# Attention decode, layer 2: scores of eight kept heads laid out as 256 keys on 128 partitions instead of 512 keys on 64

## The chip, the cores and the metric

The kernel runs on one core of one Trainium2 chip. The metric is device time of one execution in microseconds (us). The span in the profile goes from the first to the last instruction of one profiled execution; the execution's time has a little more around it.

## The reference

Two layers, each an attention block (A) and an MLP mixer (B), for a single token `x` of 640 values. Both layers use the same weights and the same cache.

```python
def _A_ref(x, k_cache, v_cache, wq, wo):          # 32 heads of 192, cache 32768 long
    W = min(4096, max(256, Sk // 4))               # 4096: the last 4096 keys
    q = (x @ wq) per head
    k, v = k_cache[:, :, Sk - W:, :], v_cache[:, :, Sk - W:, :]
    p = softmax(einsum("bhqd,bhkd->bhqk", q, k) * Dh ** -0.5)
    return einsum("bhqk,bhkd->bhqd", p, v) per token @ wo

x = x + _A_ref(layernorm(x), ...)                  # layer 1 (layer == 0 in the code)
x = x + _B_ref(layernorm(x), ...)
x = x + _A_ref(layernorm(x), ...)                  # layer 2 (layer == 1 in the code)
x = x + _B_ref(layernorm(x), ...)
```

Each head of K or V in the window is 4096 x 192 bf16, 1.5 MB. One query reads all of them once per layer, so the work is mostly the reading of the cache from HBM.

## The kernel before

**Loads.** Everything big is loaded by DMAs that SP issues in one fixed order (`stream`, `layer_stream`), mostly 1.5 MB each (`load_wide`, L55). They land in twelve cells of SBUF. `take` hands out the cell that has been free longest, `give` returns one; a load into a cell waits on SP's queue until the last reader of the cell has finished, and everything behind it in that queue waits too. The loads of a layer follow the work: K of the next group of four heads between the V of the current one, then a block of `wo`.

**Kept data.** The K of heads 0 to 7, already turned, stays in eight cells from layer 1 to layer 2 (`kept`, `NKEEP = 8`), with one V (head 2), one V in PSUM and in other spare places (head 3), most of the V of head 4 in `kl` and `kx`, and one block of `wo`. Layer 2 therefore begins with V of heads 0 and 1 as its only new loads: the K of head 8 goes into the cell of the first kept head to be scored, the part of V of head 4 that was not kept into the second, K of head 9 into the third, and so on. Layer 1 runs its groups of four heads from the last to the first, layer 2 from the first to the last.

**Scores.** K comes in with 128 partitions of 32 keys each. VectorE turns it in place in 32x32 blocks (`transpose_half`, L441, two halves per head). `scores` then does, per head, `NCOL` = 6 blocks of the head's values times `NT` = 2 strips of matmuls (L526): each reads a block of 16 columns of `Qblk` as weights and streams 512 columns of K, taking every second element, and writes 16 of the 32 PSUM partitions of its strip. The four heads of a group add up into the same place, each with its own rows. So the scores of a group are 64 partitions x 512. `ST_both` is one PSUM bank of 128 x 512; `next_scores` gives its lower and its upper 64 partitions in turn, so that the next group can be scored while the current one is in softmax.

**Softmax of a group** (`softmax_steps`): `part_max` (L552, VectorE) per partition; `turn_max` (L557, TensorE) into one row; `full_max` (L562, L565); `spread_max` (L573 TensorE, L576 and the exp L579 on ScalarE, into bf16 in `o_sb`); `turn_p` (L585, VectorE turns P in blocks, onto the other 64 partitions; L587); `swap` (L599, eight matmuls that bring P into the layout for P times V, L602 copy, L607 sum); `recip` (L614, L616).

**P times V** (`pv`, L649) per head: 16 matmuls of 384 columns, on four strips of 32 PSUM partitions in turn; then a turn (L656) and `o_fold` (L663, L664). `out_proj` (L677) or `out_row` (L695) is the product with `wo`.

**Order.** The order on TensorE, VectorE, ScalarE and SP is the order of the program (`manual_schedule`). In layer 2 the query of heads 0 to 3 is projected in two halves (`qa`, `qb`, L472 to L510), head 0 is scored, the second half is finished, heads 1 to 3 are scored with the softmax scale (L410, `softmax_scale`) behind head 1 and the next query's projection behind head 2. Then, for `gi == 0`, heads 4 to 7 are scored between the softmax steps of heads 0 to 3. For `gi == 1`, the softmax of heads 4 to 7 runs, and the scores of head 8, the first head whose K was loaded in this layer, stand between `spread_max` and the projection of the following query:

```python
                    turn_max()
                    full_max()
                    spread_max()
                    S(h0, 1, ST_n, 0)
                    h1 = nxt[1][1]
                    q = None
                    if gi + 2 < len(groups):
                        q = qproj_steps(...)
                    if q:
                        q[0]()
```

Of the kernel before, what the change touches and what calls it, by code (L numbers as in the profile page):

```python
# [10 lines left out]
F32 = mybir.dt.float32  # L11
# [7 lines left out]
P = 128  # L19
# [13 lines left out]
NJ4, NGK, NM = 4, 8, 4  # L33
# [26 lines left out]
def kernel(  # L60
# [14 lines left out]
    nc = tc.nc  # L75
# [12 lines left out]
    QH = 4  # L88
# [3 lines left out]
    NT = 2  # L92
    HP = P // 2
# [35 lines left out]
    psm = ctx.enter_context(tc.tile_pool(name="psm", bufs=2, space=PSUM))  # L129
# [219 lines left out]
    Eq = Ei.rearrange("p (j b) -> p j b", j=4)  # L349
# [165 lines left out]

    def scores(h, K, ST, hq):

        ng = NGK // NT
        Q = [Qblk[:, h // QH % 2, QAT[hq] + n * QSTEP:][:, 0:QW] for n in range(NCOL)]
        T = K.rearrange("p (j g f i t) -> p g j f i t", j=NJ4, g=NGK, f=NFB, t=2)  # L520
        for f in range(NFB):
            for t in range(2):
                n = 2 * f + t
                for i in range(NT):
                    r = ST[0] + 32 * i
                    nc.tensor.matmul(  # L526
                        ST_both[r:r + QW, :].rearrange("p (g j i) -> p g j i", g=ng, j=NJ4), lhsT=Q[n],
                        rhs=T[:, ng * i:ng * (i + 1), :, f, :, t],
                        start=(hq == 0 and n == 0), stop=(hq == QH - 1 and n == NCOL - 1))

# [2 lines left out]
    nc.vector.memset(ST_both[:], 0.0)  # L533
    turn = [0]

    def next_scores():
        turn[0] += 1
        i = turn[0] % 2 * HP
        return i, ST_both[i:i + HP, :]

    def softmax_steps(n, ST, sc, space, bank=None):

        held = {}
        halves = space.bitcast(BF16)
        at, ST_ps = ST
        S, T = slice(at, at + HP), slice(HP - at, P - at)

        def part_max():  # L550
            pm = short("pm")
            nc.vector.tensor_reduce(out=pm[S, :], in_=ST_ps, op=ALU.max, axis=AX.X)  # L552
            held["pm"] = pm

        def turn_max():
            pmT_ps = psm.tile([1, HP], F32, tag="psm")
            nc.tensor.transpose(pmT_ps[0:1, :], held["pm"][S, 0:1], ident[S, S])  # L557
            held["pmT"] = pmT_ps

        def full_max():  # L560
            ngm = space[0:1, 256:256 + 2 * QH]
            nc.vector.tensor_reduce(out=ngm[:], in_=held["pmT"][0:1, :].rearrange("o (q x m) -> o x q m", q=NT, m=NM),  # L562
                                    op=ALU.max, axis=AX.XY, negate=True)
            wide = space[0:1, 306:306 + HP]
            nc.vector.tensor_scalar(  # L565
                out=wide.rearrange("o (q x m) -> o q x m", q=NT, m=NM),
                in0=ngm[:].unsqueeze(1).unsqueeze(3).broadcast_to([1, NT, 2 * QH, NM]),
                scalar1=sc[0:1, 0:1], scalar2=None, op0=ALU.mult)
            held["w"] = wide

        def spread_max():
            nb_ps = psm.tile([P, 1], F32, tag="psm")
            nc.tensor.matmul(nb_ps[S, :], lhsT=held["w"],  # L573
                             rhs=one[0:1, :], start=True, stop=True)
            nb_sb = space[S, 289:290]
            nc.scalar.copy(nb_sb[:], nb_ps[S, :])  # L576
            Pr = halves[S, 0:SW]
            lpart = space[S, 288:289]
            nc.scalar.activation(out=Pr, in_=ST_ps, func=ACTF.Exp,  # L579
                                 bias=nb_sb[:, 0:1], scale=sc[S, 0:1], accum_out=lpart[:, 0:1])  # L580
            held["Pr"], held["l"] = Pr, lpart

        def turn_p():
            held["PrT"] = halves[T, 0:SW]
            nc.vector.transpose(held["PrT"], held["Pr"])  # L585
            lh = space[S, 280:284]
            nc.vector.tensor_scalar(out=lh[:], in0=hm[S, :], scalar1=held["l"][:, 0:1], scalar2=None, op0=ALU.mult)  # L587
            held["lh"] = lh

        def swap():  # L590
            ng = NGK // NT
            if bank is None:
                PT_ps = psm.tile([P, n, NJ4, NGK], F32, tag="psm")
            else:
                PT_ps = bank[:, 0:n * NJ4 * NGK].rearrange("p (h j g) -> p h j g", j=NJ4, g=NGK)
            src = held["PrT"].rearrange("p (g j i) -> p i j g", g=ng, j=NJ4)
            for m in range(NM):
                for q in range(NT):
                    nc.tensor.matmul(PT_ps[32 * m:32 * (m + 1), :, :, ng * q:ng * (q + 1)], lhsT=Eq[T, (HP - at) // 32 + q, :],  # L599
                                     rhs=src[:, m:QW:NM], start=True, stop=True)  # L600
            PT = big.tile([P, n, NJ4 * NGK], BF16, name="PT")
            nc.scalar.copy(PT[:].rearrange("p h c -> p (h c)"), PT_ps[:].rearrange("p h j g -> p (h j g)"))  # L602
            if bank is None:
                l_ps = psm.tile([P, QH], F32, tag="psm")
            else:
                l_ps = bank[:, 512:512 + QH]
            nc.tensor.matmul(l_ps[:], lhsT=ones[S, :], rhs=held["lh"][:], start=True, stop=True)  # L607
            held["lps"] = l_ps
            return PT

        def recip():
            lq = space[:, 284:288]
# [108 lines left out]
    def attention(layer, x_cur, rs_cur, x_new, z_new, rs_new, ss_new):  # L721
# [56 lines left out]
        for step in qa[1:]:  # L778
            step()
        qb[1]()  # L780
        ST = next_scores()
        q1 = qproj_steps(groups[1][0] // QH, xc)
        for hq, h in enumerate(groups[0]):
            for half in range(2):
# [30 lines left out]
        for gi, cur in enumerate(groups):  # L815
# [6 lines left out]
            if nxt:  # L822
                part_max, turn_max, full_max, spread_max, turn_p, swap, recip = softmax_steps(
                    len(cur), ST, sc, o_words, V_bank if layer == 1 and gi > 0 else None)
                ST_n = next_scores()
                if layer == 1 and gi == 0:

                    keep = [hh for hh in nxt if hh[1] < NKEEP]
# [23 lines left out]
                else:  # L852
# [7 lines left out]
                    turn_max()  # L860
                    full_max()
                    spread_max()
                    S(h0, 1, ST_n, 0)
                    h1 = nxt[1][1]
                    q = None
                    if gi + 2 < len(groups):
# [4 lines left out]
                    if layer == 1:  # L871
                        turn_p()
                        PT = swap()
                    if pending is not None:
                        y_ps = out_row(layer, *pending, acc, gi - 1 == rows[0]) if in_row else out_proj(layer, pending)
                    if layer == 0:
# [249 lines left out]
```

## Time and profile before

| | |
|---|---|
| median of 3 runs | 513.82 us (513.09 to 517.1) |
| the profiled execution | 513.58 us, its span 511.7 us |
| mean granted TensorE clock | 0.722 |
| DMA queue q1, share of 16 engines | 98.2%, 214.02 MB |
| busy: TensorE / VectorE / ScalarE | 293.1 (57%) / 297.4 (58%) / 52.1 us (10%) |
| scores, L526 | 768 matmuls of 512 columns, 151.1 us busy |
| turning K, L441 | 112 of 1759 ns, 194.6 us busy |
| P times V, L649 | 968 records, 90.3 us busy |
| exp, L579 / maximum, L552 / turn of P, L585 | 773 / 674 / 706 ns each |

In a row of a group or of the timeline, the line number, the engine, the operation and the tiles (`out<-in`) are given; "x12" is how many instructions the row holds. In a row of a stretch of time, the columns are the stretch, its length, and for TensorE's matmuls, its weight loads, VectorE, ScalarE and GpSimd the busy us with the number of instructions; then the granted clock as a share of full speed, the busy share of the 16 DMA engines (it can pass 1 in a short stretch, since packets are counted whole) and the GB/s that ended in it. The layer boundary is near 286 us of the span: the last product of the first mixer (L1070) ends at 286.4, and the first scores of layer 2 begin at 288.75.

### The profile page before, as it was taken

What the parts mean: (1) busy time and instruction counts of PE and PEld (TensorE: products, weight loads), DVE (VectorE), ACT (ScalarE), POOL (GpSimd) and SP (SyncE); (2) the same over time, 40 slices, a digit from 0 to 9 for tenths busy, and PEclk for the clock granted to TensorE, in tenths of its full rate; (3) what the DMA queues carried; (4) which work ended last, traced back from release to release, by engine and by line L of the source; (5) the groups of instructions that cost most, each with busy time, mean ns of one, the idle gap of its engine ahead of it and who ended that gap; (6) DMA issues with size and microseconds to landing.
All of it is one profiled execution on the core that took longest, in us unless ns stands there. A gap on an engine that the chain in (4) does not pass through costs nothing. (4 is left out here: it accounts for less than half of the span.)

```text
span 511.7 us, 7558 instructions
## 1 busy us (share of the span) xinstructions
PE 293.1 (57%) x3188; PEld 141.8 (28%) x3188; DVE 297.4 (58%) x492; ACT 52.1 (10%) x173; POOL 3.7 (1%) x16
## 2 busy tenths in 40 slices
PE   1145747546275463855665885848474762726585
PEld 0011313213132231422232432414231331312254
DVE  2086686557574584567633236776777475656622
ACT  1000101010010101001010111011110101001101
POOL 2000000000000000000000000000000000000000
PEclk9995685858767686585665597775869596787855
DMA  8999999999999999999999999999999999999995
GB/s 369 430 430 428 430 444 430 439 430 412 454 432 409 438 420 424 432 417 453 428 376 413 369 422 428 437 430 439 427 416 439 438 425 430 417 433 432 423 409 215
DMA packets 12005, 214.50 MB, mean 419 GB/s; under 512 B 2564, under 2 KB 3076, under 8 KB 7428
## 3 DMA queue, kind: packets, MB, share of 16 engines
q1 hardware_dynamic: 11972, 214.02, 98.2%
q8 instruction: 25, 0.41, 0.3%
q14 instruction: 8, 0.07, 0.0%
HBM read 214.01 MB, written 0.00 MB: 418 GB/s over the span
## 5 line engine op out<-in xcount | busy, mean ns | idle before, releaser
L441 DVE STREAM_TRANSPOSE cell<-cell 128x1536 uint32<-128x1536 uint32 x112 | 194.6, 1759 | 35.5 <-DMA cell<-in_A_k_cache_dram 34.9
L526 PE MATMUL ST_ps<-cell,Qblk 128*16 128x512 bf16 x768 | 151.1, 507 | 71.4 <-DVE cell L441 53.8
L649 PE MATMUL O_ps<-cell,PT 128*2 128x384 bf16 x968 | 90.3, 405 | 8.3 <-DMA cell<-in_A_v_cache_dram 7.6
L526 PEld LDWEIGHTS <-Qblk 128*16 128x16 bf16 x768 | 45.3, 105 | 145.0 <-issue 123.4
L656 DVE STREAM_TRANSPOSE o_sb<-O_ps 128x384 f32<-128x384 f32 x62 | 35.0, 565 | 45.3 <-PE O_ps L649 45.3
L649 PEld LDWEIGHTS <-PT 128*2 128x2 bf16 x1024 | 36.7, 90 | 29.4 <-issue 21.5
L486 DVE TENSOR_TENSOR o_sb<-qT_ps,words 128x24 bf16<-128x24 f32 (+1 forms) x18 | 3.2, 179 | 51.1 <-PE qT_ps L482 28.9
L557 PE MATMUL pmT_ps<-ident,words 64*1 64x64 f32 x16 | 4.0, 252 | 48.7 <-DVE words L552 48.7
L585 DVE STREAM_TRANSPOSE o_sb<-o_sb 64x512 bf16<-64x512 bf16 x15 | 10.6, 706 | 24.6 <-ACT o_sb L579 24.6
L664 ACT ACTIVATE words<-oT_ps,words 32x6 bf16<-32x6 f32 x40 | 10.3, 257 | 143.0 <-PE oT_ps L663 83.1
L663 PE MATMUL oT_ps<-o_sb,Lq 128*32 128x6 f32 x160 | 12.5, 186 | 11.8 <-DVE o_sb L656 11.3
L573 PE MATMUL nb_ps<-words,o_sb 1*64 1x1 f32 x30 | 4.9, 230 | 24.8 <-DVE o_sb L565 24.8
L663 PEld LDWEIGHTS oT_ps<-o_sb,Lq 128*32 128x32 f32 x160 | 10.9, 128 | 22.4 <-issue 15.6
L461 PE MATMUL qr_ps<-wq_sb,words 128*1 128x384 bf16 x90 | 15.8, 514 | 0.0
L557 PEld LDWEIGHTS pmT_ps<-ident,words 64*1 64x1 f32 x16 | 1.2, 76 | 51.7 <-issue 51.7
L669 ACT ACTIVATE words<-oT_ps,words 32x6 bf16<-32x6 f32 x24 | 6.2, 257 | 92.1 <-PE ST_ps L526 64.3
L472 PE MATMUL qT_ps<-words,wq_sb 128*128 128x1 bf16 x210 | 7.2, 165 | 13.0 <-DMA wq_sb<-in_A_wq_dram 12.2
L552 DVE TENSOR_REDUCE words<-ST_ps 64x1 f32<-64x512 f32 x16 | 10.8, 674 | 5.0 <-PE ST_ps L526 4.9
L695 PE MATMUL yr_ps<-cell,words 128*1 128x320 bf16 x108 | 13.4, 406 | 0.0
L576 ACT COPY o_sb<-nb_ps 64x1 f32<-64x1 f32 x15 | 2.3, 153 | 95.3 <-PE nb_ps L573 95.3
L573 PEld LDWEIGHTS nb_ps<-words,o_sb 1*64 1x64 f32 x30 | 4.0, 189 | 27.8 <-issue 26.2
L579 ACT ACTIVATE o_sb<-ST_ps,o_sb,words 64x512 bf16<-64x512 f32 x15 | 11.6, 773 | 0.5
(161 smaller groups left out, 202.7 us busy)
## 6 DMA issues: line engine op xcount, KB each, us to landing
cell<-in_A_k_cache_dram SPq DMA_DIRECT2D x56, 1536.0 KB, 27.7
cell<-in_A_v_cache_dram SPq DMA_DIRECT2D x56, 1536.0 KB, 27.7
cell<-in_A_wo_dram SPq DMA_DIRECT2D x13, 960.0 KB, 27.7
wq_sb<-in_A_wq_dram SPq DMA_DIRECT2D x5, 1536.0 KB, 13.5
cell<-in_A_v_cache_dram SPq DMA_DIRECT2D x6, 768.0 KB, 23.7
cell<-in_B_w_dram SPq DMA_DIRECT2D x1, 1536.0 KB, 12.6
cell<-in_B_w_dram SPq DMA_DIRECT2D x2, 768.0 KB, 10.3
cell<-in_A_wo_dram SPq DMA_DIRECT2D x3, 480.0 KB, 17.0
```

Source lines behind the costliest of these rows:

```text
L441: nc.vector.transpose(Ku, Ku)
L461: nc.tensor.matmul(qr_ps[32 * i:32 * i + 1, :], lhsT=xc[:, kc:kc + 1], rhs=wq_sb[:, kc, t0 * P + i * N:t0 * P + (i + 1) * N], start=(kc == ...
L526: nc.tensor.matmul(ST_both[r:r + QW, :].rearrange("p (g j i) -> p g j i", g=ng, j=NJ4), lhsT=Q[n], rhs=T[:, ng * i:ng * (i + 1), :, f, :, ...
L552: nc.vector.tensor_reduce(out=pm[S, :], in_=ST_ps, op=ALU.max, axis=AX.X)
L573: nc.tensor.matmul(nb_ps[S, :], lhsT=held["w"], rhs=one[0:1, :], start=True, stop=True)
L579: nc.scalar.activation(out=Pr, in_=ST_ps, func=ACTF.Exp, bias=nb_sb[:, 0:1], scale=sc[S, 0:1], accum_out=lpart[:, 0:1])
L585: nc.vector.transpose(held["PrT"], held["Pr"])
L649: nc.tensor.matmul(O_ps[r:r + 2, :], lhsT=PT[:, hq, 2 * i:2 * i + 2], rhs=v_pair(V, h, 2 * i * Dh, 2 * Dh), start=(i < 4), stop=(i >= NB - 4))
L656: nc.vector.transpose(o_sb[:], O_ps.rearrange("p (e a c) -> p e c a", e=2, c=NA))
L663: nc.tensor.matmul(oT_ps[r, :], lhsT=Lq[:], rhs=o_sb[:, e, :, e], start=(e == 0), stop=(e == 1))
L664: nc.scalar.activation(oT[r, :], oT_ps[r, :], ACTF.Copy, scale=rl[r, 0:1])
L695: nc.tensor.matmul(yr_ps[32 * i:32 * i + 1, :], lhsT=oT[:, k:k + 1], rhs=wo_t[:, k * D + i * N:k * D + (i + 1) * N], start=(k == 0), stop= ...
```

## The change

For the scores of heads 0 to 3 and of heads 4 to 7 in layer 2, `next_scores` is called with 4 strips instead of 2. A strip then holds 256 keys' columns, the scores of a group are 128 partitions x 256, and the two groups have the left and the right 256 columns of the bank. Per head there are 24 matmuls of 256 columns instead of 12 of 512. The softmax steps work on 128 partitions with half the columns; P is turned in place (onto the same partitions, next to itself); `swap` has 16 matmuls instead of 8, each of half the columns. All other groups keep 64 partitions x 512. Since the scores of heads 8 to 11 (64 partitions x 512) overlap those of heads 4 to 7 (128 x 256) in the bank, the scores of head 8 move from behind `spread_max` to behind `turn_p` and `swap` (`late`).

```diff
     def scores(h, K, ST, hq):
-        ng = NGK // NT
+        at, ST_ps, nt = ST
+        ng = NGK // nt
...
-                for i in range(NT):
-                    r = ST[0] + 32 * i
+                for i in range(nt):
+                    r = 32 * i
                     nc.tensor.matmul(
-                        ST_both[r:r + QW, :].rearrange("p (g j i) -> p g j i", g=ng, j=NJ4), lhsT=Q[n],
+                        ST_ps[r:r + QW, :].rearrange("p (g j i) -> p g j i", g=ng, j=NJ4), lhsT=Q[n],
                         rhs=T[:, ng * i:ng * (i + 1), :, f, :, t],
...
-    def next_scores():
+    def next_scores(nt=NT):
         turn[0] += 1
-        i = turn[0] % 2 * HP
-        return i, ST_both[i:i + HP, :]
+        if nt == NT:
+            i = turn[0] % 2 * HP
+            return i, ST_both[i:i + HP, :], nt
+        i = turn[0] % 2 * SW // 2
+        return 0, ST_both[:, i:i + SW // 2], nt
...
-        at, ST_ps = ST
-        S, T = slice(at, at + HP), slice(HP - at, P - at)
+        at, ST_ps, nt = ST
+        np_, w = 32 * nt, 2 * SW // nt
+        S = slice(at, at + np_)
+        T, t_at = (slice(HP - at, P - at), (HP - at) // 32) if nt == NT else (S, 0)
...
-            pmT_ps = psm.tile([1, HP], F32, tag="psm")
+            pmT_ps = psm.tile([1, np_], F32, tag="psm")
...
-            wide = space[0:1, 306:306 + HP]
+            wide = space[0:1, 306:306 + HP] if nt == NT else space[0:1, w // 2:w // 2 + np_]
...
-            Pr = halves[S, 0:SW]
+            Pr = halves[S, 0:w]
...
-            held["PrT"] = halves[T, 0:SW]
+            held["PrT"] = halves[T, 0:w] if nt == NT else halves[T, w:2 * w]
...
-            ng = NGK // NT
+            ng = NGK // nt
...
-                for q in range(NT):
-                    nc.tensor.matmul(PT_ps[...], lhsT=Eq[T, (HP - at) // 32 + q, :],
+                for q in range(nt):
+                    nc.tensor.matmul(PT_ps[...], lhsT=Eq[T, t_at + q, :],
...
-        ST = next_scores()
+        ST = next_scores(4 if layer == 1 else NT)
...
-                ST_n = next_scores()
+                ST_n = next_scores(4 if layer == 1 and gi == 0 else NT)
...
                     spread_max()
-                    S(h0, 1, ST_n, 0)
+                    late = layer == 1 and gi == 1
+                    if not late:
+                        S(h0, 1, ST_n, 0)
...
                     if layer == 1:
                         turn_p()
                         PT = swap()
+                    if late:
+                        S(h0, 1, ST_n, 0)
```

More of the change, by code (lines that the diff above doesn't have):

```diff
@@ L561, in full_max @@
             ngm = space[0:1, 256:256 + 2 * QH]
-            nc.vector.tensor_reduce(out=ngm[:], in_=held["pmT"][0:1, :].rearrange("o (q x m) -> o x q m", q=NT, m=NM),
+            nc.vector.tensor_reduce(out=ngm[:], in_=held["pmT"][0:1, :].rearrange("o (q x m) -> o x q m", q=nt, m=NM),
                                     op=ALU.max, axis=AX.XY, negate=True)
-            wide = space[0:1, 306:306 + HP]
+            wide = space[0:1, 306:306 + HP] if nt == NT else space[0:1, w // 2:w // 2 + np_]
             nc.vector.tensor_scalar(
-                out=wide.rearrange("o (q x m) -> o q x m", q=NT, m=NM),
-                in0=ngm[:].unsqueeze(1).unsqueeze(3).broadcast_to([1, NT, 2 * QH, NM]),
+                out=wide.rearrange("o (q x m) -> o q x m", q=nt, m=NM),
+                in0=ngm[:].unsqueeze(1).unsqueeze(3).broadcast_to([1, nt, 2 * QH, NM]),
                 scalar1=sc[0:1, 0:1], scalar2=None, op0=ALU.mult)
@@ L597, in swap @@
             for m in range(NM):
-                for q in range(NT):
-                    nc.tensor.matmul(PT_ps[32 * m:32 * (m + 1), :, :, ng * q:ng * (q + 1)], lhsT=Eq[T, (HP - at) // 32 + q, :],
+                for q in range(nt):
+                    nc.tensor.matmul(PT_ps[32 * m:32 * (m + 1), :, :, ng * q:ng * (q + 1)], lhsT=Eq[T, t_at + q, :],
                                      rhs=src[:, m:QW:NM], start=True, stop=True)
```

## The prediction

> **What bounds the kernel now.** I read first the page, for what is busy; then stretches of time with their DMA rate, for where loads were missed; last the timeline and SP's own waits at the one place that the change can reach.
>
> The span is 511.7 us, and the transfers fill nearly all of it:
>
> ```profile
> DMA  8999999999999999999999999999999999999995
> GB/s 369 430 430 428 430 444 430 439 430 412 454 432 409 438 420 424 432 417 453 428 376 413 369 422 428 437 430 439 427 416 439 438 425 430 417 433 432 423 409 215
> ...
> q1 hardware_dynamic: 11972, 214.02, 98.2%
> ```
>
> At the 430 GB/s of most slices, 214.02 MB take 497.7 us. The other 14 us of the span are the start, the end (the last row of the second layer's mixer lands near 504.9, and 6.8 us of work follow) and the slices that are short. So an edit is worth what it changes in the stream of loads: time in which no load was in the queue, or the end behind the last one. Two slices in the middle, 376 and 369, are short. Finer stretches show where:
>
> ```profile
> 265.00:270.00 5.00, 3.52 (x60) 2.31 (x57) 1.41 (x5) 0.52 (x2) 0.00 (x0) 0.50 0.86 313
> ...
> 290.00:295.00 5.00, 5.00 (x39) 1.73 (x36) 0.43 (x3) 0.47 (x2) 0.00 (x0) 0.82 0.80 310
> 295.00:320.00 25.00, 16.84 (x223) 7.92 (x223) 12.96 (x29) 3.33 (x11) 0.00 (x0) 0.85 1.02 425
> 320.00:345.00 25.00, 15.47 (x206) 7.96 (x204) 18.58 (x26) 2.31 (x8) 0.71 (x2) 0.77 1.02 440
> 345.00:450.00 105.00, 63.67 (x640) 28.97 (x637) 70.49 (x98) 11.45 (x35) 0.00 (x0) 0.72 1.00 430
> ```
>
> (The last three columns are the granted clock, the DMA share and GB/s.) The dip at 265 lies in the first layer's last group, which the change leaves alone. The dip at 290 is the start of the second layer. Behind 295 the rate is whole again to the end phase: there the queue always holds a load, and a cell that comes free sooner buys nothing. By single microseconds the dip is this:
>
> ```profile
> 289.00:290.00 1.00, 1.00 (x8) 0.28 (x6) 0.00 (x0) 0.00 (x0) 0.00 (x0) 0.50 1.03 430
> 290.00:291.00 1.00, 1.00 (x8) 0.27 (x4) 0.00 (x0) 0.00 (x0) 0.00 (x0) 0.50 1.00 418
> 291.00:292.00 1.00, 1.00 (x9) 0.30 (x7) 0.27 (x2) 0.00 (x0) 0.00 (x0) 0.58 0.67 283
> 292.00:293.00 1.00, 1.00 (x12) 0.28 (x6) 0.00 (x0) 0.00 (x0) 0.00 (x0) 1.00 0.58 188
> 293.00:294.00 1.00, 1.00 (x10) 0.58 (x10) 0.00 (x0) 0.44 (x2) 0.00 (x0) 1.00 0.94 307
> 294.00:295.00 1.00, 1.00 (x14) 0.30 (x9) 0.15 (x1) 0.03 (x1) 0.00 (x0) 1.00 0.84 356
> 295.00:296.00 1.00, 1.00 (x34) 0.84 (x34) 0.17 (x1) 0.00 (x0) 0.00 (x0) 1.00 0.97 381
> ```
>
> 288 to 291 ran at 414 GB/s on average. From 291 to 296 the five rows move 1515 KB where 5 x 414 = 2070 would have fitted: 555 / 414 = **1.3 us lost**. The cause is a load that came late:
>
> ```profile
> 288.75 2.73 PE L526 MATMUL ST_ps<-cell,Qblk 128*16 128x512 bf16 x12 [0.27 <-DVE Qblk L510]
> ...
> 291.51 0.33 SPq L157 DMA_DIRECT2D cell<-in_A_k_cache_dram  x1
> ...
> 291.53 1.65 PE L526 MATMUL ST_ps<-cell,Qblk 128*16 128x512 bf16 x12
> ...
> 293.22 0.33 SPq L182 DMA_DIRECT2D cell<-in_A_v_cache_dram  x1
> ```
>
> and among the SP queue's waits from 286 to 307 (us in total, times, longest):
>
> ```profile
> SPq L157 <- PE Qrep_ps L493: 5.4, 1, 5.4
> ```
>
> The first load of K for head 8 needs a cell. Ten of the twelve hold kept data when layer 2 begins (eight turned K, one V, one block of wo) and two take the V of heads 0 and 1. The next cell comes free when kept head 0 has been scored, at 291.48; SP had waited 5.4 us for PE, and issues at 291.51, when the load before has almost drained. The wait is named after Qrep_ps, the PE instruction behind the scores.
>
> **The change, part by part.** *Scores of the eight kept heads (L526).* Per head 12 matmuls of 512 columns become 24 of 256; the columns streamed are the same 6144, but on four strips of 32 PSUM partitions instead of two. How wide do strips run side by side? In the first head the weight loads of a pair start 0.427 us apart (289.14, 289.56, 289.99): six pairs make 2.56, and with 0.17 for the end the 2.73 of the row. So two strips of 512 columns share 0.427 us at clock 0.50. The nearest row with four strips is L649: sixteen matmuls of 384 columns take 1.45 us at the same clock, their weight loads in fours 0.32 us apart (263.98, 264.30). Per column and strip 0.427/512 and 0.32/384 are the same 0.83 ns: four run as freely as two there. So six fours of 256 columns take 6 x 0.213 = 1.28, plus 0.17: **1.45 us instead of 2.73**, 1.28 saved at half clock. At full clock a head takes 1.46 us from its first matmul to the next user of PE (295.72 to 297.19); halved in the same way that is about 0.82, or by an issue bound from L677 (30 weight load and matmul pairs of one column in 0.90, 30 ns a pair, so 24 x 0.030 = 0.72, plus 0.17) 0.89. What the rows don't show is four strips with 16 weight columns and every second element read, as K is. Bounds: 1.45 us if they run as L649's do; 2.73 if only two run at once (12 pairs of 0.213, plus 0.17), no gain; 4.4 if each pair's weight loads stand ahead of it uncovered (0.14 us for two in the first head: 12 x 0.354, plus 0.17), a loss of 1.7. I take 1.45: in both shapes the weight loads lie inside the stream already.
>
> The Trainium skill, in "TensorE: Matmul & The Clock Gate", section "Measured speedup vs the span model", gives 3.07 times for four packed row tiles and 2.38 for three column tiles, less than the count. By 3.07 of 4 the first head would take about 1.8 us and the load would gain 0.9 rather than 1.28, so 512.7 by my sum. L649's 0.32 us per four shows the whole factor here, with column strips back to back; I go by the row.
>
> *The late load.* Its issue moves from 291.51 to 290.23. In the trace the rate falls about half a microsecond behind the issue and is recovered two later, so a load issued at 290.23 is moving before the one ahead drains. What is won is not above the 1.3 lost and not above the 1.28 of the earlier issue: I take **1.2**, since some of the loss is the slow first packets of each load.
>
> *The next loads.* Heads 1 to 7 end earlier by a sum that grows: 1.28 + 0.2 for the second head (half its columns at half clock) and 0.6 for each of six, near 5 us by the eighth. The load behind head 1 moves from 293.22 to about 291.7. All wait behind the first in a queue that runs at 425 GB/s from 295 on, so nothing is counted; without that cover the gain could grow by 25 x (1 - 425/430) = 0.3 us.
>
> *Softmax of the two groups on 128 x 256.* The maximum (L552, 674 ns for 64x512), exp (L579, 773) and the turn of P (L585, 706) read half the columns. Bounds for each: half and the whole; near 0.4, 0.5 and 0.4. The one-row steps double (L562 0.21, L565 0.24 for 64 values, so up to 0.9 together instead of 0.45), `swap` issues 16 matmuls instead of 8 (0.44 us, at most 0.88) with half the columns. Net between a gain of 1.0 and a loss of 0.9 per group, all of it on DVE, ACT and PE behind 295, where the stream covers it. No DMA is added.
>
> *The moved scores of head 8 (`late`).* With group 1 on all 128 partitions, the next scores write over columns that exp reads, so `S(h0, 1, ST_n, 0)` goes behind `turn_p` and `swap`. Before, it ran from 319.18 to 321.91, and the SP issue at 321.95 followed. Now PE does the projection first (0.95), waits for the turn of P, and does `swap` (up to 0.88) and the sum behind the cast (0.65): the scores end some 1.7 us later against the rest of the group, and behind them stand out_proj and PV, which keep their order and lose nothing in sum. SP's queue is held 1.7 us longer for that cell, but the group starts up to 5 us earlier. Nothing is late next while the loads queued there last: 6.8 us separate the issues at 315.13 and 321.95, and 320 to 345 still runs at 440 GB/s. Were that cover gone, it would cost its 1.7: 514.1.
>
> *The end.* From the last landing near 504.9 to 511.7 no instruction changes.
>
> **Sum.** The profiled execution took 513.58 us (span 511.7, 1.9 around it). 513.58 - 1.2 = 512.4. Its own time is 0.24 below the median of the three runs, 513.82, which run from 513.09 to 517.1; so a median of new runs may stand at 512.6 as well.
>
> **The rivals.** *A. The gap stays.* Four strips that read every second element of K are throttled to two, or the first load's lateness was its own start and not the cell. For it: no row shows this shape. Against it: SP's 5.4 us wait on PE. Time: 513.6, with the softmax's small change hidden.
>
> *B. The clock was not at half.* The granted clock turns to 1.00 inside 291 to 292. In executions where it turns 3 us earlier, head 0 needs 1.46 before and 0.85 after; the load comes 0.6 earlier into a gap of that size or less: 513.1. For it: the clock in the page's PEclk line changes between slices at no fixed place. Against it: PE is busy 0.73 to 0.74 of 286 to 289, and the clock is still 0.50.
>
> *C. Slower: weight loads uncovered.* 24 instead of 12, each for all 128 rows, each ahead of only 0.213 us of streaming. From the bound above head 0 ends 1.7 us later, at 293.15; the dip grows by 1.7. At full clock a head then takes 12 x (0.107 + 0.14) + 0.17 = 3.1: head 1 ends near 296.3, head 2 near 299.6, but its load is needed at 298.7 (3.7 for the first and 0.9 for the short second, from 294.1) and moves a microsecond after its issue: 1.9 more. 513.6 + 3.6 = 517.2. It decides once a four takes over 0.427 us. Against it: 0.427 and 0.32 us are the bare streams in both shapes, so the loads hide there. The same page of the Trainium skill ("Packing small matmuls", "The mechanism") says that a weight load overlaps running matmuls only where its row group differs; here all use all rows, and by that rule C holds. L526 and L649 also use all rows, and their weight loads lie inside the streams; the trace does not agree with it for column strips.
>
> *D. More than the dip.* A gain above 1.6 us needs a stretch behind 295 in which loads are missed. The rows leave 0.3. About 511.5, from that and the scatter of runs.
>
> **How the numbers follow.** Forecast 0.70, A 0.14, B 0.08, C 0.05, D 0.03. The predicted time is the forecast's 512.4, own range 511.8 to 513.0. The range takes in A and B and the half microsecond by which undisturbed runs differ from the profiled one: 511.2 to 514.6; C and part of D lie outside. About 1% (5 us) is what a measurement of this kernel can tell from no change. Faster by that would need 508.4, when bytes, start and end alone make 498 + 2 + 7 = 507: 0.01. Slower by that would need 518.7, beyond C, so only something I have not seen: 0.03. Within: 0.96.
>
> **What would show it.** Right: in the changed profile the first twelve matmuls of L526 in layer 2 are twenty-four in about 1.45 us at half clock; the L157 load of K issues 1.3 us sooner against the first scores; the DMA rate stays near 410 across the place of the dip; eight heads end about 5 us sooner while the last landing moves by 1.2 only. Wrong: a first head over 2 us, a dip of the old depth, a new dip where head 8 is scored late, or a stretch behind the dip that runs above 430.

## The result, and the profile after

The changed kernel takes 512.63 us in the median of ten executions (511.19 to 513.72), the kernel before 514.16 beside it (512.78 to 517.1). The ratio is 0.9962 [0.9944, 0.9981]: 2.0 us less, somewhere between 1.0 and 2.9 (the two medians are 1.5 apart). Run again beside 35 executions of the kernel before (median 513.54), the change gave 512.12 and 0.9977 [0.9959, 0.9995], that is 1.2 us less. Both intervals hold the predicted gain of 1.2 us. The profiled execution took 512.68 us with a span of 510.9, where 512.4 had been predicted.

Line numbers behind L526 shift: the scores are L527 now, the maximum L559, exp L586, the turn of P L592, `swap` L606. First the page of the changed kernel, the slices of the DMA and its queue:

```profile
DMA  9999999999999999999989999999999999999995
GB/s 370 431 431 428 431 441 435 436 435 413 439 433 409 435 426 439 428 408 463 428 358 413 387 451 425 424 431 428 436 427 434 432 432 431 417 443 428 417 406 217
...
q1 hardware_dynamic: 11972, 214.02, 98.4%
```

The bytes are the same. (A rate in these views counts a packet whole in the stretch in which it starts, not where it ends, as was said further up; the packets of the wide loads hold 48 KB and take 1.82 us, so a row of one microsecond is rough.) The slice with the start of layer 2 reads 387 where it read 369, and the one behind it 451 instead of 422; the slice with the first layer's dip is a little worse (358 for 376). Then stretches of the changed kernel, with the columns as before (the last three are the granted clock, the DMA share and GB/s):

```profile
290.00:295.00 5.00, 4.89 (x118) 3.05 (x106) 0.68 (x5) 0.47 (x2) 0.00 (x0) 0.80 0.98 350
295.00:320.00 25.00, 17.34 (x341) 10.23 (x343) 15.28 (x34) 3.19 (x12) 0.71 (x2) 0.85 1.02 431
320.00:345.00 25.00, 15.52 (x187) 7.89 (x188) 17.69 (x23) 3.25 (x10) 0.00 (x0) 0.77 1.01 436
```

290 to 295 moved at 310 GB/s and moves at 350 now; the engines' share there went from 0.80 to 0.98. The long rows behind 295 are alike: 431 and 436, where 425 and 440 stood. Shorter ones are not. The kernel before has a second dip just behind 295, which its row from 295 to 320 hides (the second hole that the experiments speak of is another one, behind 300). First its rows, then those of the change:

```profile
295.00:300.00 5.00, 3.88 (x56) 1.87 (x54) 1.20 (x4) 0.00 (x0) 0.00 (x0) 1.00 1.05 386
300.00:305.00 5.00, 3.86 (x39) 1.58 (x37) 2.45 (x6) 1.10 (x4) 0.00 (x0) 1.00 1.11 476
```

```profile
295.00:300.00 5.00, 3.43 (x92) 2.58 (x93) 2.38 (x9) 0.81 (x3) 0.00 (x0) 1.00 1.14 468
300.00:305.00 5.00, 3.24 (x86) 2.09 (x90) 4.61 (x12) 0.27 (x1) 0.00 (x0) 1.00 1.02 437
```

In these ten microseconds the kernel before moves 4310 KB and the change 4525, half a microsecond's worth more. The first dip by single microseconds, in the change:

```profile
291.00:292.00 1.00, 1.00 (x21) 0.43 (x13) 0.00 (x0) 0.00 (x0) 0.00 (x0) 0.51 1.30 418
292.00:293.00 1.00, 1.00 (x26) 0.75 (x26) 0.11 (x1) 0.47 (x2) 0.00 (x0) 1.00 0.96 238
293.00:294.00 1.00, 1.00 (x40) 0.93 (x38) 0.04 (x1) 0.00 (x0) 0.00 (x0) 1.00 0.80 320
294.00:295.00 1.00, 0.90 (x25) 0.50 (x17) 0.25 (x2) 0.00 (x0) 0.00 (x0) 1.00 0.88 369
295.00:296.00 1.00, 0.36 (x16) 0.40 (x19) 0.59 (x3) 0.00 (x0) 0.00 (x0) 1.00 0.99 393
```

This dip is shallower, not gone. 291 to 296 move 1738 KB, where the prediction's measure is 5 x 414 = 2070: 332 / 414 = 0.8 us are still lost, where 1.3 were. In the timeline of the changed kernel stand the new scores and the load that the first of them release:

```profile
289.01 1.46 PE L527 MATMUL ST_ps<-cell,Qblk 128*16 128x256 bf16 x24 [0.27 <-DVE Qblk L510]
...
290.52 0.33 SPq L157 DMA_DIRECT2D cell<-in_A_k_cache_dram  x1
...
293.89 0.88 PE L527 MATMUL ST_ps<-cell,Qblk 128*16 128x256 bf16 x24
...
300.19 0.89 PE L527 MATMUL ST_ps<-cell,Qblk 128*16 128x256 bf16 x24
```

Kept head 0 takes 1.46 us for 24 matmuls at clock 0.50, a head at full clock 0.88 (where the row said 1.53 before). The K of head 8 is issued 1.51 us behind the first scores instead of 2.76. The last row is head 7: it ends at 301.1, 12.1 us behind the first scores, where it ended 17.9 behind them before (near 5 us sooner had been worked out; it is 5.8). Among SP's waits of the changed kernel (us in total, times, longest), from 250 to 345, the one for this load is:

```profile
SPq L157 <- PE Qrep_ps L493: 4.1, 1, 4.1
```

It was 5.4. The softmax of the two groups has these rows among the groups of 286 to 330 (busy us, mean ns of one):

```profile
L586 ACT ACTIVATE o_sb<-ST_ps,o_sb,words 128x256 bf16<-128x256 f32 x2 | 1.1, 564 | 0.1
...
L592 DVE STREAM_TRANSPOSE o_sb<-o_sb 128x256 bf16<-128x256 bf16 x2 | 0.9, 446 | 2.8 <-ACT o_sb L586 2.8
...
L559 DVE TENSOR_REDUCE words<-ST_ps 128x1 f32<-128x256 f32 x2 | 0.8, 399 | 0.0
```

From the start of the first scores of layer 2 to the end of the span, the measure that leaves out how the first layer went, the profiles have 222.95 us before and 221.89 after.

### The profile page after: what moved, and what is told of

Its sections match the earlier page's. It is cut to its first block, busy times and chain, and to the rows that moved or that the text cites. A ratio compares the mean times of both kernels' runs of the same rounds, so it can differ in the third digit from the quotient of the medians.

```text
span 510.9 us, 7784 instructions
## 1 busy us (share of the span) xinstructions
PE 282.8 (55%) x3300; PEld 141.3 (28%) x3300; DVE 296.1 (58%) x492; ACT 51.8 (10%) x173; POOL 3.7 (1%) x16
## 4 chain that ended last, share of the span: by engine, by line
DMA 73%; PE 11%; DVE 11%; issue 2%; ACT 2%; SPq 1%; ACTq 0%
DMA cell<-in_A_v_cache_dram 38%; DMA cell<-in_A_k_cache_dram 31%; DVE cell L441 7%; PE ST_ps L527 5%; DMA cell<-in_B_w_dram 4%; PE O_ps L656 1%; DVE o_sb L663 1%; ACT o_sb L586 1%; PE y_ps L1081 1%; PE qT_ps L472 1%; DVE words L559 1%; DVE V_ps L645 1%; PE qr_ps L461 1%; SPq L55 0%; DVE Qblk L510 0%
## 5 line engine op out<-in xcount | busy, mean ns | idle before, releaser
L527 PE MATMUL ST_ps<-cell,Qblk 128*16 128x512 bf16 (+1 forms) x864 | 143.9, 468 | 76.4 <-DVE cell L441 60.4
L656 PE MATMUL O_ps<-cell,PT 128*2 128x384 bf16 x968 | 88.4, 398 | 7.9 <-DMA cell<-in_A_v_cache_dram 6.0
L527 PEld LDWEIGHTS <-Qblk 128*16 128x16 bf16 x864 | 45.1, 103 | 146.5 <-issue 124.3
L564 PE MATMUL pmT_ps<-ident,words 64*1 64x64 f32 (+1 forms) x16 | 4.0, 253 | 51.3 <-DVE words L559 51.2
L592 DVE STREAM_TRANSPOSE o_sb<-o_sb 64x512 bf16<-64x512 bf16 (+1 forms) x15 | 10.1, 671 | 23.6 <-ACT o_sb L586 23.6
L580 PE MATMUL nb_ps<-words,o_sb 1*64 1x1 f32 (+1 forms) x30 | 5.0, 234 | 25.0 <-DVE o_sb L572 25.0
L461 PE MATMUL qr_ps<-wq_sb,words 128*1 128x384 bf16 x90 | 13.9, 463 | 0.0
L559 DVE TENSOR_REDUCE words<-ST_ps 64x1 f32<-64x512 f32 (+1 forms) x16 | 10.2, 640 | 3.8 <-PE ST_ps L527 3.7
L583 ACT COPY o_sb<-nb_ps 64x1 f32<-64x1 f32 (+1 forms) x15 | 2.3, 154 | 94.0 <-PE nb_ps L580 94.0
L580 PEld LDWEIGHTS nb_ps<-words,o_sb 1*64 1x64 f32 (+1 forms) x30 | 4.2, 193 | 27.6 <-issue 26.0
L586 ACT ACTIVATE o_sb<-ST_ps,o_sb,words 64x512 bf16<-64x512 f32 (+1 forms) x15 | 11.2, 746 | 0.5
```

What stands on the lines that cost most here:

```text
L461: nc.tensor.matmul(qr_ps[32 * i:32 * i + 1, :], lhsT=xc[:, kc:kc + 1], rhs=wq_sb[:, kc, t0 * P + i * N:t0 * P + (i + 1) * N], start=(kc == ...
L527: nc.tensor.matmul(ST_ps[r:r + QW, :].rearrange("p (g j i) -> p g j i", g=ng, j=NJ4), lhsT=Q[n], rhs=T[:, ng * i:ng * (i + 1), :, f, :, t] ...
L586: nc.scalar.activation(out=Pr, in_=ST_ps, func=ACTF.Exp, bias=nb_sb[:, 0:1], scale=sc[S, 0:1], accum_out=lpart[:, 0:1])
L656: nc.tensor.matmul(O_ps[r:r + 2, :], lhsT=PT[:, hq, 2 * i:2 * i + 2], rhs=v_pair(V, h, 2 * i * Dh, 2 * Dh), start=(i < 4), stop=(i >= NB - 4))
```

## The experiments

**Theory:** the time is set by the stream of loads. The only thing that the change moves in it is the issue of the K of head 8, through the scores of kept head 0; the rest of the change is hidden. **Rivals:** the gain comes from the other shortened heads or the cheaper softmax and not from this load; or the hole in the stream is no loss at all, since the stream makes it good. Below, "K issue" is how long behind the first scores of layer 2 the K of head 8 is issued, and "to the end" goes from those first scores to the end of the span.

### The change again, and the load made late on purpose

The change unaltered:

> The changed kernel as it is, run beside the next three so that they can be set against it. Theory (the whole gain is the load of K of head 8, issued sooner, in a hole of the load stream): ratio to before 0.996 to 0.999, and from the first scores of layer 2 to the end of the span 1.0 to 1.3 us less than before's 222.95. Rival (the gain grows with the five microseconds by which the later heads end sooner, or is spread over the stages behind): more than 1.6 us less, or stretches behind 300 us with a rate above 431 GB/s.

Measured: 0.9977 [0.9959, 0.9995], K issue 1.50 us, 221.29 to the end. That is 1.7 us less than 222.95, above the 1.0 to 1.3 expected and just over the 1.6 named as the rival's sign; 300 to 305 ran at 434 GB/s, over the rival's 431 as well. Against the second profile of the kernel before (222.53, told of below) it is 1.2. So this run does not set the theory apart from the rival that the gain is spread over the heads behind. In this execution the granted clock stayed at 0.50 from 290 to 315, so all eight heads took 1.46 us each, and the time is no worse for it: what the heads save at full clock was not needed for the gain here.

Ten matmuls whose result nothing reads, ahead of the first scores:

```diff
+        if layer == 1:
+            pad_ps = psm.tile([P, 512], F32, tag="psm")
+            for i in range(10):
+                nc.tensor.matmul(pad_ps[0:32, :], lhsT=Eq[:, 0, :], rhs=wq_sb[:, 0, 0:512], ...)
         ST = next_scores(4 if layer == 1 else NT)
```

> Ten matmuls of 512 columns that nobody reads stand on TensorE ahead of the first scores of layer 2: at half clock up to 4.3 us, of which some 0.3 is hidden and some runs at full clock; all heads of the two groups still end sooner against each other than before's. Theory: the load of head 8's K is issued 3 to 4 us later than in the changed kernel, at about 294, the stream runs dry from about 292 to 295, and the time rises by nearly the same, 2.5 to 3.7 us over the changed kernel: the load has no slack. Rival (the gain lies in the later heads, and the first load only fills up what the stream could make good later): less than 1 us over the changed kernel.

Measured: 514.18 us, 1.0023 [1.0006, 1.004]; 2.1 us above the change in the medians, 2.3 in the spans. That is less than the 2.5 to 3.7 expected, and well over the rival's 1. The K of head 8 is issued at 293.32. The same single microseconds of this kernel:

```profile
291.00:292.00 1.00, 1.00 (x13) 0.38 (x12) 0.00 (x0) 0.00 (x0) 0.00 (x0) 0.50 0.44 176
292.00:293.00 1.00, 1.00 (x20) 0.54 (x18) 0.00 (x0) 0.00 (x0) 0.00 (x0) 0.73 0.09 37
293.00:294.00 1.00, 1.00 (x28) 0.62 (x25) 0.27 (x2) 0.00 (x0) 0.00 (x0) 1.00 0.00 0
294.00:295.00 1.00, 1.00 (x30) 0.81 (x26) 0.00 (x0) 0.43 (x2) 0.00 (x0) 1.00 0.93 160
295.00:296.00 1.00, 1.00 (x42) 0.76 (x30) 0.15 (x1) 0.03 (x1) 0.00 (x0) 1.00 0.80 319
```

The stream runs dry, and most of what it loses there reaches the end (1378 KB too little against 2070, 3.3 us, where the second profile of the change lost 0.3); the rival that the stream makes it good falls. The ten matmuls hold up every head and load behind them too, but counted packet by packet the loss lies in the first 8 us behind the first scores (3.5 of 3.6 us), before the next loads are due. The rows also show what a load needs when nothing is ahead of it: issued at 293.32, its first packet starts at 294.28, 160 GB/s in the microsecond from 294, 319 in the next, 406 from 296 on. Its first thirteen packets take 1.0 to 1.3 us each, later ones of the same 12 KB 0.46. The full rate comes some 2.7 us behind the issue. That would explain the dip that is left after the change: the load is issued at 290.52, the ones ahead end near 292, and the rate is low until the new one is up.

### An extra load into the hole

480 KB that nobody needs, loaded between the V of head 1 and the K of head 8, in the kernel before and in the changed one. By itself it takes 480 / 430 = 1.1 us of the stream:

```diff
+        if (layer, h) == (1, NKEEP):
+            src = A_v_cache[0, VX, s0:Sk, :].rearrange("(p j) d -> p (j d)", p=P)
+            nc.sync.dma_start(kl[:], src[:, FREE - VN:FREE - NKX * Dh])
         t = take(("k", layer, h))
```

> The kernel before with one more load: 480 KB of V of head 4 are loaded again into the place where they already lie (kl), issued by SP just ahead of the load of head 8's K, where it waits for nothing. It is 0.23% more bytes, 1.14 us of stream at 430 GB/s. Theory: the stream has a hole of 1.3 us at that place, so the load runs in the hole and costs 0 to 0.3 us. Rival (no real hole: the low rate comes from the form of the loads around it): it costs its full 1.1 us.

> The same extra load of 480 KB in the changed kernel, in which the load of head 8's K comes before the stream is dry. Theory: the hole is closed, so it costs 0.7 to 1.1 us from the first scores of layer 2 to the end (the lower value if the slow first packets of K of head 8 leave part of the hole). Rival: as in the kernel before, 0 to 0.3.

Measured: in the kernel before 513.21 us, 0.9998 [0.9979, 1.0016], and 222.69 to the end, where the two profiles of that kernel (the second is told of below) have 222.95 and 222.53. The extra load costs nothing that can be seen, and by the interval less than its full 1.1 us. Its profile shows that it fills the hole: counted packet by packet, the twelve microseconds from the first scores on lose 0.7 us against 430 GB/s, where the two profiles of the kernel before lose 2.2 and 1.8. But it also shows a second hole, of 1.2 us, further on:

```profile
305.00:310.00 5.00, 4.73 (x77) 2.30 (x75) 3.73 (x13) 0.27 (x1) 0.00 (x0) 1.00 0.91 315
```

The granted clock rose late in this execution (5.6 us behind the first scores, where it was 3.1 and 3.4 in the two profiles of the kernel before), and the load that waits for head 5 was issued 14.0 us behind them instead of 12.9 and 13.0. So what the extra load costs by itself is not cleanly shown.

In the changed kernel 512.75, 0.9986 [0.9968, 1.0003]: 0.6 us above the change in the medians of the same comparison, and to the end 222.19, which is 0.3 above the first profile of the change and 0.9 above the second. That is less than the full 1.1; 0.9 lies inside the 0.7 to 1.1 expected, 0.3 at the edge of the rival. Counted packet by packet, the twelve microseconds from the first scores on lose 0.4 us here, where the two profiles of the change lose 1.2 and 0.9. The stretches of the changed kernel with the extra load:

```profile
291.00:292.00 1.00, 1.00 (x14) 0.81 (x18) 0.00 (x0) 0.43 (x2) 0.00 (x0) 0.50 1.10 445
292.00:293.00 1.00, 1.00 (x27) 0.47 (x16) 0.15 (x1) 0.03 (x1) 0.00 (x0) 0.53 0.89 326
293.00:294.00 1.00, 1.00 (x42) 0.94 (x42) 0.18 (x1) 0.00 (x0) 0.00 (x0) 1.00 1.04 442
294.00:295.00 1.00, 0.66 (x21) 0.33 (x12) 0.30 (x3) 0.00 (x0) 0.00 (x0) 1.00 1.10 471
295.00:296.00 1.00, 0.60 (x24) 0.55 (x24) 0.35 (x2) 0.00 (x0) 0.00 (x0) 1.00 1.01 430
```

With the extra load these five microseconds move 2114 KB: next to no hole is left. Without it the first profile of the change moves 1738 KB there (0.8 us lost), the second 1928 (0.3 lost). 1.1 less these is 0.3 and 0.8, and the two measures to the end show 0.3 and 0.9; with one execution each, that may be chance. So, by the profiles, the change fills the hole in part, and how much is left differs between executions; the interval of the ratio is too wide to say it of the times.

### One group alone

The two groups with four strips separately. Since the two shapes overlap in the bank, the scores of heads 4 to 7 here wait for the exp of the first group (the softmax steps up to `spread_max` stand ahead of head 4), in both kernels. First, four strips for heads 0 to 3 alone:

```diff
-                ST_n = next_scores(4 if layer == 1 and gi == 0 else NT)
+                ST_n = next_scores()
...
-                    between = [lambda: (turn_max(), full_max()), spread_max, turn_p, lambda: None]
+                    turn_max()
+                    full_max()
+                    spread_max()
+                    between = [turn_p, lambda: None, lambda: None, lambda: None]
...
-                    late = layer == 1 and gi == 1
+                    late = False
```

> Only heads 0 to 3 of layer 2 are scored on four strips. Heads 4 to 7 go back to two strips on 64 partitions; since these overlap the first group's 128 x 256 in the bank, they are scored behind the first group's maximum and exp, which puts them some 3 us later against head 3, and head 8 is scored at its old place. Theory: the load of head 8's K is issued 1.5 us behind the first scores as in the changed kernel, and the whole gain is there: ratio to before 0.996 to 0.999, from the first scores to the end 221.2 to 222.0 us. Rival (each head that is scored faster brings its part): half the gain or none, since heads 4 to 7 end no sooner than before.

Measured: 513.87 us, 1.0005 [0.999, 1.002], 222.37 to the end, though the K issue is at 1.51 us. The theory missed, and the rival's forecast came true: the load that the theory calls the whole cause comes early, and the gain is not there. The profiled execution was the fastest of its kernel (512.06, as fast as the change) and shows no new hole (447 and 413 GB/s in 300 to 305 and 305 to 310).

Four strips for heads 4 to 7 alone (`ST = next_scores()` for the first group, the same order):

> The other half alone: heads 0 to 3 on two strips as before, heads 4 to 7 on four strips behind the first group's exp, head 8 behind `swap`. Theory: the load of head 8's K is issued 2.76 us behind the first scores as before, the hole is there, and nothing is gained: ratio 0.999 to 1.001, from the first scores to the end 222.6 to 223.2 us. Rival: half the gain.

Measured: 513.66 us, 1.0 [0.9979, 1.0021], K issue 2.76 us, 223.16 to the end. The second group's shape gains nothing alone, as expected.

To see what took the gain of the first group, that kernel was profiled once more:

> The kernel with four strips for heads 0 to 3 alone once more, for a second profile: the profiled execution of the first, at 512.06 us, was the fastest of its twelve, whose median was 513.87. Theory: in a usual execution the load behind head 5, issued late because its heads wait for exp, finds the stream dry: a second hole of 0.5 to 2 us between 300 and 310, seen by a DMA rate under 400 GB/s there, and worse where the granted clock is at half. Rival: no second hole, the time lies elsewhere.

Measured: 513.68 us in this one execution, near the median of the twelve, and here the profile has a second hole. In its timeline the three heads 4 to 6 and the load that waits for head 5:

```profile
298.64 6.38 PE L527 MATMUL ST_ps<-cell,Qblk 128*16 128x512 bf16 x36 [0.94 <-ACT o_sb L586]
...
303.70 0.47 SPq L55 DMA_DIRECT2D cell<-in_A_k_cache_dram  x1
```

and its stretches:

```profile
300.00:305.00 5.00, 5.00 (x44) 1.83 (x44) 2.38 (x4) 0.00 (x0) 0.00 (x0) 0.68 0.91 379
305.00:310.00 5.00, 4.16 (x87) 2.19 (x77) 2.02 (x7) 0.27 (x1) 0.00 (x0) 1.00 1.07 383
```

The load that waits for head 5 comes at 303.70, 14.8 us behind the first scores (13.6 in the execution without a hole), 8.5 us behind the load ahead of it, and 300 to 310 fall under 385 GB/s; counted packet by packet the hole costs 1.5 us. With the changed kernel the same load is issued at 297.57. So the early heads 4 to 7 are not idle gain: they keep that load from being late. That a second hole took the gain in the other executions as well is likely, but only these two were profiled.

### The second hole made on purpose

Twenty matmuls that nothing reads, between the maximum of the first group and the scores of head 4, in the kernel before and in the changed one:

```diff
                     part_max()
+                    pad_ps = psm.tile([P, 512], F32, tag="psm")
+                    for i in range(20):
+                        nc.tensor.matmul(pad_ps[0:32, :], lhsT=Eq[:, 0, :], rhs=wq_sb[:, 0, 0:512], ...)
                     between = [...]
```

> Twenty matmuls of 512 columns that nobody reads, in the kernel before, between the first group's maximum and the scores of head 4: 4.3 us of TensorE at full clock, some 0.5 of it hidden. It stands for an execution in which the later heads are slow. Theory now: the loads that wait on heads 4 to 7 have little slack in the kernel before (the one behind head 5 is issued at 301.65 and is needed near 305), so a second hole opens: 0.7 to 2.5 us more than before. Rival (only the first load counts): 0 to 0.3 us.

> The same twenty matmuls at the same place in the changed kernel, in which these loads are issued 4 to 5 us sooner: the one behind head 5 at 297.57, needed near 304.5. Theory: within 0.5 us of the changed kernel, so what the faster later heads bring is slack that pays only in executions where they are slow. Rival (that slack is worth time in every execution): 1 us or more over the changed kernel.

Measured: in the kernel before 514.87 us, 1.0022 [1.0006, 1.0038], 225.12 to the end; that load is issued at 304.89 instead of 301.65, and its stretches have the hole:

```profile
300.00:305.00 5.00, 5.00 (x36) 1.95 (x35) 0.46 (x2) 0.00 (x0) 0.00 (x0) 1.00 1.05 452
305.00:310.00 5.00, 3.86 (x44) 1.66 (x43) 3.31 (x6) 1.28 (x4) 0.00 (x0) 1.00 0.88 318
```

In the changed kernel 513.16, 0.9991 [0.9972, 1.0009]. Its load is issued at 301.06 and the same two stretches run at 423 and 408 GB/s: no second hole in the profile. By the ratio it still stands 0.7 us above the change (0.9977), between the two expectations and inside the intervals, and its 222.82 to the end is 0.9 and 1.5 above the two profiles of the change. So the profile shows that the changed kernel bears this delay better; that its time bears it wholly is not shown.

### The moved scores, and the clock

The scores of head 8 at their old place (`late = False` in the changed kernel and nothing else; TensorE then waits there until exp has read the bank):

> The changed kernel with the scores of head 8 at their old place, behind `spread_max`; they wait there for exp, about 1 us, as they did before. Theory: the queue holds over 5 MB of loads at that time, so it doesn't matter: within 0.5 us of the changed kernel. Rival (the moved scores hold back a cell, or spare TensorE a wait that counts): 1 us or more either way.

Measured: 511.93 us, 0.9974 [0.9961, 0.9987], the same as the change. Where head 8 is scored makes no difference that can be seen.

Three dense matmuls that nothing reads, ahead of the last product of the first mixer, to have the clock raised before head 0:

> The changed kernel with three matmuls of 512 columns that nobody reads, in the gap of TensorE ahead of the first mixer's last product (1.7 us idle in the trace), to have the granted clock up before the first scores. Theory: if the clock is at 1.00 by then, head 0 takes about 0.9 us instead of 1.46, the load comes 0.6 us sooner and takes at most the 0.3 to 0.4 us that are left of the hole; if it stays at 0.50, nothing changes. Rival (the clock at the layer's start is worth more than that, since all eight heads run at it): over 1 us less than the changed kernel.

Measured: 512.44 us, 0.9977 [0.9964, 0.999], the same as the change; but head 0 still took 1.46 us at clock 0.50. The clock was not raised, so the run tells nothing on what head 0 would bring at full clock.

A last look at the kernel before:

> The kernel before once more, for a second profile: the hole behind the first head's scores is again there, about 1.3 us between the layer's first scores and eight microseconds later. Theory: if the granted clock stays at half behind the first head here, a second hole follows behind 300; if it rises as in the first profile, none.

Measured: 513.32 us, K issue 2.77 us; the clock rose at 292 as in the first profile, 222.53 to the end. The first hole is there (176 GB/s from 293 to 294; in all 0.7 to 0.8 us by the same measure, where the first profile lost 1.3), the second hole, behind 300, is not. It was to show an execution of the kernel before at half clock throughout, as the change had one, and did not.

## Why the prediction was right, and where it was not

**Scores of a head: right.** 1.46 us measured for 1.45 predicted at half clock. At full clock a head takes 0.82 us to the next user of PE (293.89 to 294.71), the way in which the prediction had measured 1.46; that is its halved value, and less than its issue bound of 0.89. Four strips that read every second element with 16 weight columns run as L649's do. C falls with this row, and of A the throttling to two strips; A's other half, that the load's lateness is its own start, fits the part of the dip that stayed. The Trainium skill ("TensorE: Matmul & The Clock Gate", section "The mechanism") says that a weight load overlaps running matmuls only where its row group differs; by that alone the kernel would have been slower. 24 weight loads of all 128 rows fit into these 1.46 us, so the trace does not agree with it for column strips. The same section of the Trainium skill also lets a weight load go ahead when it targets the background weight buffer, which the prediction left out; no run here tells whether that is what happens. An estimate from the 3.07 that the same page of the Trainium skill gives for four row tiles (section "Measured speedup vs the span model") would have been 1.8 us.

**The issue of the load: right.** 1.25 us sooner against the first scores (1.51 for 2.76), in every kernel with four strips for heads 0 to 3 and nothing put ahead of them.

**The gain of 1.2 us: right in size, partly by luck.** The ratios say 2.0 and 1.2 us, each about a microsecond either way. The prediction had all of it come from the K of head 8 and nothing from the loads behind it. The traces divide it otherwise. Here each packet's bytes are spread over the time that it took, and the table has the microseconds lost against 430 GB/s, from the first scores of layer 2 on, in two profiles of each kernel:

| | 0 to 8 us | 8 to 12 us | 12 to 210 us |
|---|---|---|---|
| before | 1.5, 1.2 | 0.7, 0.6 | 0.0, 0.0 |
| change | 1.1, 0.8 | 0.1, 0.1 | 0.1, 0.1 |

So the first dip, the one that the prediction is about, became some 0.4 us shallower in the mean, not 1.2, and the second dip behind it, which the prediction does not have, brought near 0.6. Together that is near 1.0; that it lies so close to 1.2 is luck.

The sentence "a load issued at 290.23 is moving before the one ahead drains" did not hold. The load that was forced late needs some 2.7 us to the full rate, and the changed kernel gives it about 1.5 before the others end, so "the DMA rate stays near 410 across the dip" was wrong. The bound "not above the 1.3 lost" was wrong too: it was read from five microseconds in which packets are counted whole, while the start of layer 2 lost 2.2 and 1.8 us in the two profiles.

Behind 210 us, in the end phase with the work behind the last load, the loss by the same measure is 6.4 and 5.9 us before and 6.2 and 5.6 in the change: it differs between executions of one kernel by as much as between the kernels. That is why the profiles, to the end of the span, stand anywhere from 0.6 to 1.7 us apart.

**The next loads, counted at nothing: wrong.** The prediction took "behind 295 the rate is whole again" from a row of 25 us (425 GB/s), and that row holds the second dip. There the load of the K of head 9 starts, which waits for head 2. Before, it is issued 6.2 and 6.4 us behind the first scores; in the change 4.2 and 4.9, since heads 0 to 2 are shorter. In the two profiles of the kernel before, the fifteen packets of 48 KB that start 8 to 11 us behind the first scores took 2.3 and 2.4 us on average; in the change the packets of this size there took the usual 1.8. That is the mark of a load that starts late, as in the run with the ten matmuls. All five profiles with two strips for heads 0 to 3 lose 0.25 to 0.73 us in this stretch, all nine with four strips 0.19 or less. No run moves this load alone, so that its lateness makes the dip is inferred, not shown. The rival that part of the gain comes from the other shortened heads therefore stands.

Further on the cover that the prediction named (the queue behind 295 is full) depends on heads 4 to 7 ending early: with the first group alone the load that waits for head 5 came 14.8 us behind the first scores in the second profile, with a hole of 1.5 us, and the gain was gone. In the changed kernel it comes at 8.6 us at full clock and 11.2 at half clock. In the kernel before it comes at 12.9 and 13.0, without a hole; with the extra load and a late clock it came at 14.0, with one. How often executions of the kernel before have such a hole is not known.

**Softmax: right and hidden.** 0.40, 0.56 and 0.45 us for maximum, exp and turn; `swap` took 0.46 us for 16 matmuls where up to 0.88 had been allowed.

**`late`: right.** Head 8's scores start at 314.37 instead of 319.18, since the group starts earlier, and their place costs nothing that can be seen.

**B and D.** The clock was at half for head 0 in both profiles, so B's condition did not occur. D asked for a stretch behind 295 in which loads are missed, and there is one, but only of 0.6 to 0.7 us. D's 511.5 lies inside the first comparison's interval; the repeat, and two variants of the change at 0.9974 and 0.9977, speak for 1.2.

## What to carry to other kernels

In a kernel bound by its loads, look for the loads that wait for an engine longer than the queue lasts; what sits ahead of their release is worth time, and what the stream covers is not. Go through the loads behind the first late one too, one by one, in stretches no longer than one load takes, before counting them at nothing: here a row of 25 us hid a dip that was worth half of the gain. An extra load put into a suspected hole can measure it, if the loads behind it are watched as well. When the first late release is mended, work out the slack of the next ones, at the lowest clock that the profile shows: the part of a change that gains nothing alone may be what keeps the next hole shut.

## What the hardware showed that was not expected

A load issued into a drained queue moved nothing for 0.96 us (293.32 to 294.28), its first packets took 1.0 to 1.3 us instead of 0.46, and it came to the full rate about 2.7 us behind its issue. The rate fell in the changed kernel although SP had issued some 1.5 us before the queue ended.

The granted clock differs between executions of one kernel over the same work: with the change it rose to 1.00 at 292 in the first profile and stayed at 0.50 from 290 to 315 in the second, with no cost to the time (510.9 and 509.9 us of span). Three dense matmuls ahead of head 0 did not raise it.
